# Sums inverted in slot 9, transposes one slot earlier, and the end of attention reordered: a fused attention and MoE kernel

## The chip, the cores and the metric

The kernel runs on one NeuronCore of a Trainium2 chip. Its engines run their own instruction streams in order and wait for one another by semaphores: TensorE (PE; PEld is its weight load), VectorE (DVE), ScalarE (ACT), GpSimd (POOL) and SyncE (SP), which here issues nearly all DMA transfers. The metric is the device time of one execution in microseconds; before the change the median of three runs is 876.56 us (876.08 to 878.52).

## The reference

```
q_assign = argmax(q_n . c_n);  k_assign = argmax(k_n . c_n)      # 16 clusters per head
mask     = q_assign == k_assign
scores   = where(mask, q k^T / sqrt(D), -1e9);  scores -= max(scores)
attn     = exp(scores);  attn /= sum(attn) + 1e-9;  x = attn v   # B=2, H=8, S=768, D=64
y        = relu(x w_in)^2 w_out                                  # 1536 tokens, 512 -> 2048 -> 512
out      = (h cos h) w2_out,  h = y w2_in
```

## The kernel before

**Attention.** The 16 heads are taken as eight pairs `n`, each of 768 queries by 768 keys. A pair has 12 slots (`SP`), one for each block of 128 keys (`kt`, 6) of each half of the queries (`hf`, 384 columns). Halves are numbered `hb` = 2n + hf, 0 to 15; slots run over all pairs as `g` = 0 to 95. In slot `g`:

- `scores` (L397) makes the transposed scores of one key block for both heads in eight matmuls and ScalarE takes the exponential into `p` (L413). The last two matmuls read `d["lq"]`, into whose outer rows `stage_max` has written the row maxima.
- `s_max` (L350) makes scores of the slot nine further on a second time, untransposed; VectorE takes their row maxima (L362).
- in odd slots `pv` (L427) multiplies the `p` of two earlier slots with V into `o_ps[hf]`.
- `add_up` (L415) adds the `p` of a half up in `acc`, on GpSimd, and for the very last half on VectorE.

`unit()` and `give()` hand out three PSUM units of two banks each in turn; whoever takes one waits for its last reader.

**What sets the order.** Three tables of (offset, place, function) say in which slot a step is issued and whether ahead of the slot's scores (PRE), behind its matmuls (PROD) or at its end (POST): `prep` (L806) for the preparation of a later pair, `prep_all` (L837) for the row maxima, `finish` (L846) for the end of a half. An offset in `prep` and `prep_all` counts from nine slots before the pair, one in `finish` from the half's first slot. Each engine, and SP's queue too, then works in this order.

- `prep`: load q and k (L226), transpose them (`transpose_in`, L244, six matmuls on `rawq` or `rawk`), copy (`full_copy`), round (`high_part`) and take the rest (`low_part`), then find each token's cluster (`sims`, `by_token`, `at_max`, `one_hot`) and move the operands of the second product (`stage_own`, `stage`, `stage_oh`: transfers `set<-set`, `ext<-set`, `ext<-ot`).
- `prep_all`: `stage_max` (L384) moves the row maxima of a half, `set<-mr`, two slots before that half's first.
- `finish`: `sums` (L442) sums `p` over the keys with a matrix of ones; `move_sums` (L453) copies the 128x192 result and gathers its four useful rows by four small transfers into a 64x12 tile `r`; three slots later `invert` (L473) adds 1e-9, inverts, writes `row` in DRAM and reads it back broadcast over 64 rows a head (`rb`); two slots later `divide` (L484) multiplies `o_ps` by `rb` into `x`, and `combine` (L488) splits `x` into the MoE's operands `xh` (ScalarE) and `xl` (GpSimd).

The last two halves do without DRAM: `sums_here` (L463) makes the sums on all 128 rows, `invert_here` (L470) inverts a 128x384 tile.

**MoE.** `moe` (L767) runs steps of one block of 512 tokens and one of 16 blocks of d_ff: `h_mm` (L610) and, two steps later, `y_mm` (L663), with elementwise work between. Weights are split on VectorE (L141, lines 157 to 161 and 153), two pieces in each of the last nine slots of attention and up to twelve in a step. `hooks` puts the end of attention into the first steps.

Of the kernel before, what the change touches and what calls it, by code (L numbers as in the profile page):

```python
# [9 lines left out]
F32 = mybir.dt.float32  # L10
# [4 lines left out]
AF = mybir.ActivationFunctionType  # L15
ALU = mybir.AluOpType
# [18 lines left out]
def tile_kernel(ctx: ExitStack, tc: tile.TileContext, q, k, v, centroids, w1i, w1o, w2i, w2o, out):  # L35
    nc = tc.nc
# [4 lines left out]
    P = 128  # L41
    NT = S // P
    HALF = S // 2
# [11 lines left out]
    R = D // 2  # L55
# [19 lines left out]
    eps = perm.tile([P, 1], F32, name="eps")  # L75
# [90 lines left out]
    ap = att.enter_context(tc.tile_pool(name="att", bufs=1))  # L166
# [11 lines left out]
    pairs = [(b, hp) for b in range(B) for hp in range(NP)]  # L178
    NPAIR = len(pairs)
    SP = 2 * NT  # L180
    NU = NPAIR * SP
# [7 lines left out]
    def unit():  # L189
        return free_units.pop(0)  # L190

    def give(u):
        free_units.append(u)
# [15 lines left out]
    def block(tiles, t):  # L209
        c, i = SPREAD[t]  # L210
        return tiles[c][:, S + i * P : S + (i + 1) * P]
# [138 lines left out]
    def s_max(u_):  # L350
        n, c = divmod(u_, SP)
        i, kh = divmod(c, 2)
        d = pd[n]
        u = unit()
        qs, ks = slice(i * P, (i + 1) * P), slice(kh * HALF, (kh + 1) * HALF)
        for p, (a, b) in enumerate(((d["hq"], d["hk"]), (xq[n % 2], xk[n % 2]))):
            for j in range(2):
                r = slice(j * D, (j + 1) * D)
                nc.tensor.matmul(u[:, j, :HALF], lhsT=a[r, qs], rhs=b[r, ks], start=(p == 0), stop=(p == 1))  # L359
        if c == 0:  # L360
            d["m"] = ap.tile([P, NT, 2, 2], F32, tag="m", name=f"m{n}", bufs=2)
        nc.vector.tensor_reduce(d["m"][:, i, :, kh], u[:, :, :HALF], AX, ALU.max)  # L362
        give(u)
# [30 lines left out]


    ptiles, accs = {}, {}
    def scores(u_):  # L397
        n, c = divmod(u_, SP)
        hf, kt = divmod(c, NT)
        d = pd[n]  # L400
        u = unit()
        qs, ks = slice(hf * HALF, (hf + 1) * HALF), slice(kt * P, (kt + 1) * P)
        i = n % 2
        lk, yk = d["lk"][:, ks], block(sets[n % 3], kt)
        ops = ((d["hk"][:, ks], d["hq"]), (lk, d["hq"]), (xk[i][:, ks], xq[i]), (yk, d["lq"]))
        for p, (a, b) in enumerate(ops):
            for j in range(2):
                r = slice(j * D, (j + 1) * D)
                nc.tensor.matmul(  # L409
                    u[:, j, :HALF], lhsT=a[r], rhs=b[r, qs], start=(p == 0), stop=(p == len(ops) - 1)  # L410
                )
        t = ptiles[u_] = ap.tile([P, 2, HALF], F32, tag="p", name=f"p{u_}", bufs=6)
        nc.scalar.activation(t, u[:, :, :HALF], AF.Exp, scale=SCALE)  # L413
        give(u)

    def add_up(u_):
        hb, kt = divmod(u_, NT)
        e = nc.vector if hb == 2 * NPAIR - 1 else nc.gpsimd
        if kt in (0, NT - 1):
            return  # L420
        if kt == 1:
            accs[hb] = ap.tile([P, 2, HALF], F32, tag="acc", name=f"acc{hb}", bufs=2)
        a = ptiles[u_ - 1] if kt == 1 else accs[hb]
        for j in range(2):
            e.tensor_tensor(accs[hb][:, j], a[:, j], ptiles[u_][:, j], ALU.add)  # L425
# [9 lines left out]
            )  # L435

    su, inv, rbs, xs = {}, {}, {}, {}
    GR = HALF // R
    QH = HALF // 2


# [10 lines left out]

    def move_sums(hb):  # L453
        u = su.pop(hb)
        t = ap.tile([P, QH], F32, tag="st", name=f"st{hb}")
        nc.scalar.copy(t, u[:, 0, :QH])
        give(u)
        r = inv[hb] = ap.tile([2 * R, GR], F32, tag="r", name=f"r{hb}", bufs=2)
        n = QH // GR
        for g in range(4):  # L460
            nc.sync.dma_start(r[g * n : (g + 1) * n], t[g * R : g * R + 1].rearrange("o (p c) -> o p c", c=GR))

    def sums_here(hb, u):  # L463
        for i, a in enumerate((accs.pop(hb), ptiles[NT * hb + NT - 1])):
# [5 lines left out]
    def invert_here(hb):  # L470
        nc.vector.reciprocal(rbs[hb], rbs[hb])

    def invert(hb):  # L473
        b, hp = pairs[hb // 2]
        r = inv.pop(hb)
        nc.vector.tensor_scalar(r, r, 1e-9, None, ALU.add)
        nc.vector.reciprocal(r, r)
        row = dram.tile([2, HALF], F32, tag="row", name=f"row{hb}", bufs=2)
        nc.sync.dma_start(row.rearrange("j (p c) -> (j p) c", c=GR), r)
        rb = rbs[hb] = ap.tile([P, HALF], F32, tag="rb", name=f"rb{hb}", bufs=2)  # L480
        for j in range(2):
            nc.sync.dma_start(rb[j * D : (j + 1) * D], row[j : j + 1, :].broadcast_to([D, HALF]))

    def divide(hb):  # L484
        x = xs[hb] = ap.tile([P, HALF], F32, tag="x", name=f"x{hb}", bufs=2)
        nc.vector.tensor_tensor(x, o_ps[hb % 2][:, :HALF], rbs.pop(hb), ALU.mult)  # L486

    def combine(hb):  # L488
        n, hf = divmod(hb, 2)
        b, hp = pairs[n]  # L490
        x = xs.pop(hb)
        c = hf * HALF
        while c < (hf + 1) * HALF:
            blk, off = divmod(b * S + c, TB)
            w = min((hf + 1) * HALF - c, TB - off)
            src = x[:, c - hf * HALF : c - hf * HALF + w]
            dst = xh[blk][:, hp, off : off + w]
            nc.scalar.copy(dst, src)
            nc.gpsimd.tensor_tensor(xl[blk][:, hp, off : off + w], src, dst.bitcast(F32), ALU.subtract)
            c += w  # L500

    def warm(count):
        for i in range(count):
            nc.tensor.matmul(o_ps[0][:, :P], lhsT=identb, rhs=identb, start=True, stop=True)
# [3 lines left out]
    st = prepp.tile([P, 4 * D], F32, name="st")  # L508
# [42 lines left out]
    for j in range(2):  # L551
        r = slice(j * D, (j + 1) * D)
# [214 lines left out]
    def moe(hooks):  # L767
# [36 lines left out]

    PRE, PROD, POST = range(3)
    prep = [  # L806
        (-13, PRE, load_raw, "qk"),
        (-10, PROD, transpose_in, "q"),
        (-10, POST, full_copy, "q"),
        (-9, PRE, high_part, "q"),  # L810
        (-9, POST, low_part, "q"),
        (-8, PROD, transpose_in, "k"),
        (-8, POST, full_copy, "k"),
        (-7, PRE, high_part, "k"),
        (-7, PROD, sims),
        (-7, POST, low_part, "k"),
        (-6, PROD, by_token),
        (-6, POST, stage_own),
        (-5, PROD, at_max),
# [26 lines left out]
    finish = [  # L846
        (8, PROD, sums),
        (9, PRE, move_sums),
        (12, PRE, invert),
        (14, PRE, divide),  # L850
        (14, POST, combine),
    ]
# [1 line left out]
    def run(g, where):  # L854
        for n in range(NPAIR):
            for r, w, f, *a in ([], prep_second, prep)[min(n, 2)] + prep_all:
                if g == SP * n - LEAD + r and w == where:
                    f(n, *a)
        for hb in range(2 * NPAIR - 2):
            for r, w, f in finish:  # L860
                if g == NT * hb + r and w == where:
                    f(hb)

    aux.extend(early_w.tile([P, DM], U32, name=f"aux{i}") for i in range(2))
    tops.extend(early_w.tile([P, DM], U32, name=f"top{i}") for i in range(2))
    last = 2 * NPAIR - 2
    loads = {8 * i: i for i in range(n_early)}
    loads.update({SP * (NPAIR - 2) + 1 + 2 * i: 6 + i for i in range(4)})
    loads.update({SP * (NPAIR - 1) + i: 9 + i for i in range(1, 7)})
    for g in range(-LEAD, NU):  # L870
        run(g, PRE)
        if 0 <= g < NU:
            scores(g)
        if 0 <= g + LEAD < NU:
            s_max(g + LEAD)
        if g % 2 == 1:
            for u_ in (g - 3, g - 2):
                if 0 <= u_ < NU:
                    pv(u_)
        run(g, PROD)  # L880
        run(g, POST)
        if 0 <= g - 1 < NU:
            add_up(g - 1)
        if g < -1:
            warm(WARM_STEP)
        if g in loads:
            load(0, *wanted[loads[g]], g + 4 - NU)
        if g >= SP // 2:
            if g < SP * (NPAIR - 1) - LEAD:
                count = 2 if g % SP in (1, 4, 7) else 0  # L890
            else:
                count = 2 if g >= NU - LEAD else 1
            for i in range(count):
                split_one(g - NU)
        if g == SP * (NPAIR - 1) - LEAD:
            prep_stack.close()
            mid = ctx.enter_context(tc.tile_pool(name="mid", bufs=1, side="right", reuse_waits="tile"))
            ews = mid.tile([P, 4 * TB], F32, name="ews")
            ewr = mid.tile([P, 6 * TB], F32R, name="ewr")
        if g == NU - 4:  # L900
            u = unit()
            sums_here(last, u)
            give(u)
        if g == NU - 2:
            invert_here(last)
            divide(last)
            combine(last)

    def load_mid():
        for i in wanted[16 : n_early + n_mid]:  # L910
# [2 lines left out]
    def load_late():  # L913
# [6 lines left out]

    moe({
        0: [lambda: pv(NU - 2), lambda: pv(NU - 1), lambda: sums_here(last + 1, units[2])],
        1: [load_mid],
        2: [lambda: invert_here(last + 1), lambda: divide(last + 1), lambda: combine(last + 1)],
        4: [load_late],
    })
# [28 lines left out]
```

## Time and profile before

| | us |
|---|---|
| median of 3 runs | 876.56 |
| profiled execution | 876.72 |
| its span | 875.0 |
| TensorE busy | 803.2 (92%) |
| VectorE busy | 581.7 (66%) |
| ScalarE busy | 355.7 (41%) |
| GpSimd busy | 184.4 (21%) |
| row maxima on VectorE, L362, 96 times | 91.6 |
| exponentials on ScalarE, L413, 96 times | 77.9 |

The span is the time from the first to the last instruction of one profiled execution; all times in rows count from its start. Busy time says little by itself: matmuls are pipelined, and an engine that waits in one stage and not in another has one share for both. What ended an idle stretch stands in brackets behind a row of the timeline. `SPq` rows are transfers as SyncE issues them; how long one takes to land is in the list of DMA issues.

### The profile page before, as it was taken

To read this page: it belongs to the slowest core of one execution; us is meant where nothing else is said; L and a number is where in the kernel's file an instruction comes from. 1 tells how busy PE (TensorE), PEld (TensorE's weight loads), DVE (VectorE), ACT (ScalarE), POOL (GpSimd) and SP (SyncE) were. 2 spreads that over 40 slices of the span, in tenths; PEclk is the share of its full clock that TensorE was granted. 3 is DMA by queue.
4 is the path that set the end of the run, shared out by engine and by line. 5 is a ranking of instruction groups with operands and counts; after the bars stand their busy time and mean duration, and the time that the engine had idled before them with its cause. 6 is when DMAs were issued, how large, how long until landed. Compare 5 with 4: busy or idle time off the path is not lost.

```text
span 875.0 us, 11831 instructions
## 1 busy us (share of the span) xinstructions
PE 803.2 (92%) x4453; PEld 596.8 (68%) x4453; DVE 581.7 (66%) x950; ACT 355.7 (41%) x591; POOL 184.4 (21%) x211
## 2 busy tenths in 40 slices
PE   6987977888787958999999999999899999999997
PEld 4654544545454526888888888888688888888886
DVE  5755554546555788869587731387999976667665
ACT  3344443534443433444444443444443433333332
POOL 5344445454434633200000000000222100000000
PEclk9999999999998898999999999999999999999999
DMA  4524253232314266010473000274100010001001
GB/s 109 124 76 102 55 121 87 60 91 57 83 51 133 65 210 234 2 49 1 134 227 121 1 0 1 65 228 145 46 1 0 1 49 1 0 1 49 1 0 49
DMA packets 75177, 61.84 MB, mean 71 GB/s; under 512 B 44144, under 2 KB 66416, under 8 KB 75120
## 3 DMA queue, kind: packets, MB, share of 16 engines
q1 hardware_dynamic: 73568, 60.70, 24.0%
q8 instruction: 35, 0.57, 0.3%
q10 hardware_dynamic: 1552, 0.39, 0.2%
q14 instruction: 22, 0.18, 0.1%
HBM read 47.87 MB, written 5.29 MB: 61 GB/s over the span
## 4 chain that ended last, share of the span: by engine, by line
PE 77%; DVE 7%; DMA 6%; ACT 4%; issue 2%; SPq 1%; DVEq 0%; ACTq 0%
PE unit L663 29%; PE unit L610 16%; PE o_ps L610 14%; PE o_ps L432 6%; PE unit L409 5%; DMA rb<-row 3%; PE unit L359 3%; DMA row<-r 2%; ACT p L413 2%; DVE m L362 2%; PE unit L249 1%; ACT fk L265 1%; PE unit L300 1%; PE unit L381 1%; SPq L345 1%
## 5 line engine op out<-in xcount | busy, mean ns | idle before, releaser
L610 PE MATMUL unit<-xh,w 128*128 128x512 f32 x400 | 134.3, 397 | 10.2 <-ACT p L413 6.8
L663 PE MATMUL unit<-ewr,w 128*128 128x512 f32 x576 | 141.9, 394 | 0.0
L663 PE MATMUL unit<-w,ewr 128*128 128x512 f32 x576 | 140.1, 392 | 1.8 <-ACT ewr L644 0.7
L362 DVE TENSOR_REDUCE m<-unit 128x2 f32<-128x768 f32 x96 | 91.6, 955 | 69.1 <-PE unit L359 68.3
L663 PEld LDWEIGHTS unit<-w,ewr 128*128 128x128 f32 x576 | 107.9, 188 | 26.8 <-ACT ewr L644 1.1
L663 PEld LDWEIGHTS unit<-ewr,w 128*128 128x128 f32 x576 | 107.9, 187 | 25.8
L610 PE MATMUL o_ps<-xh,w 128*128 128x512 f32 x368 | 121.2, 390 | 0.0
L413 ACT ACTIVATE p<-unit 128x768 f32<-128x768 f32 x96 | 77.9, 813 | 68.8 <-PE unit L409 66.6
L648 POOL TENSOR_TENSOR ewr<-ews,ewr 128x512 fp32r<-128x512 f32 x24 | 31.7, 1322 | 331.7 <-ACT ewr L644 297.5
L610 PEld LDWEIGHTS unit<-xh,w 128*128 128x128 f32 x400 | 76.2, 190 | 29.5 <-ACT p L413 7.4
L425 POOL TENSOR_TENSOR acc<-acc,p 128x384 f32<-128x384 f32 x90 | 92.9, 1066 | 5.6 <-ACT p L413 5.6
L409 PE MATMUL unit<-set,set 64*128 64x384 f32 x512 | 81.3, 373 | 10.3 <-ACT p L413 7.1
L648 DVE TENSOR_TENSOR ewr<-ews,ewr 128x512 fp32r<-128x512 f32 x72 | 49.5, 688 | 56.4 <-ACT ewr L627 51.4
L432 PE MATMUL o_ps<-p,rawv 128*64 128x384 f32 x384 | 82.3, 555 | 0.9 <-DVE x L486 0.8
L610 PEld LDWEIGHTS o_ps<-xh,w 128*128 128x128 f32 x368 | 69.1, 188 | 15.3
L610 PE MATMUL unit<-xl,w 128*128 128x512 f32 x200 | 79.2, 396 | 0.0
L635 ACT ACTIVATE ews<-ews,hpi 128x512 f32<-128x512 f32 x48 | 34.8, 725 | 102.9 <-DVE ews L634 102.9
L610 PE MATMUL o_ps<-xl,w 128*128 128x512 f32 x184 | 72.0, 391 | 0.0
L409 PEld LDWEIGHTS unit<-set,set 64*128 64x128 f32 x512 | 44.1, 191 | 33.2 <-ACT p L413 14.1
L359 PE MATMUL unit<-set,set 64*128 64x384 f32 x192 | 37.8, 387 | 26.2 <-DVE m L362 26.2
L153 DVE SCALAR_TENSOR_TENSOR w<-aux,aux 128x512 fp32r<-128x512 f32 x64 | 50.0, 781 | 1.8
L432 PEld LDWEIGHTS o_ps<-p,rawv 128*64 128x64 f32 x384 | 25.3, 148 | 34.4 <-issue 32.3
(129 smaller groups left out, 1072.5 us busy)
## 6 DMA issues: line engine op xcount, KB each, us to landing
wraw<-in_moe_w_in_dram SPq DMA_DIRECT2D x32, 512.0 KB, 4.5
wraw<-in_moe_w_out_dram SPq DMA_DIRECT2D x32, 512.0 KB, 4.5
rawq<-in_q_dram SPq DMA_DIRECT2D x8, 384.0 KB, 4.6
ext<-set SPq DMA_DIRECT2D x32, 96.0 KB, 2.1
rawv<-in_v_dram SPq DMA_DIRECT2D x8, 384.0 KB, 4.1
out_dram<-outs SPq DMA_DIRECT2D x12, 256.0 KB, 2.1
rawk<-in_k_dram SPq DMA_DIRECT2D x7, 384.0 KB, 5.1
rb<-row SPq DMA_DIRECT2D x28, 96.0 KB, 2.9
```

Source lines behind the costliest of these rows:

```text
L153: ve.scalar_tensor_tensor(w[:, 1], restf, 2.0**-20, power.bitcast(F32), ALU.mult, ALU.mult)
L249: nc.tensor.transpose(u[:, h, c * P : (c + 1) * P], raw[n, x][:, t].rearrange("p j d -> p (j d)"), ident)
L359: nc.tensor.matmul(u[:, j, :HALF], lhsT=a[r, qs], rhs=b[r, ks], start=(p == 0), stop=(p == 1))
L362: nc.vector.tensor_reduce(d["m"][:, i, :, kh], u[:, :, :HALF], AX, ALU.max)
L409: nc.tensor.matmul(u[:, j, :HALF], lhsT=a[r], rhs=b[r, qs], start=(p == 0), stop=(p == len(ops) - 1))
L413: nc.scalar.activation(t, u[:, :, :HALF], AF.Exp, scale=SCALE)
L425: e.tensor_tensor(accs[hb][:, j], a[:, j], ptiles[u_][:, j], ALU.add)
L432: nc.tensor.matmul(o_ps[hf][j * D : (j + 1) * D, :HALF], lhsT=raw[n, "v"][:, kt, j, :], rhs=t[:, j], start=(kt == 0), stop=(kt == NT - 1),)
L610: nc.tensor.matmul(ph, lhsT=w[:, a, :], rhs=x[blk][:, a, :], start=(a == i == 0), stop=(a == KD - 1 and i == 2))
L635: nc.scalar.activation(e2, e2, AF.Sin, bias=hpi)
L648: e.tensor_tensor(al, e2, ah.bitcast(F32), ALU.subtract)
L663: nc.tensor.matmul(y, lhsT=a, rhs=b, start=(idx in opens and i == 0), stop=(idx in closes and i == 2))
```

## The change

- `finish`: `invert` stands at the end of slot 9 of a half, not ahead of slot 12. `move_sums` writes the sums with 1e-9 added straight into a 128x192 tile `r`; the four gathering transfers, the tile `st` and the 64x12 addition are gone. `invert` inverts all 128 rows and sends every 32nd of them to `row`.
- `prep`: load, transposes, copies, rounding and rests of q and k are one slot earlier. `sims` and all behind it stay.
- `add_up`: the half last but one is added on VectorE too.
- `invert_here`, `divide` and `combine` of the half last but one move from the end of slot 94 into the MoE's step 1.

```diff
-        e = nc.vector if hb == 2 * NPAIR - 1 else nc.gpsimd
+        e = nc.vector if hb >= last else nc.gpsimd
...
     def move_sums(hb):
         u = su.pop(hb)
-        t = ap.tile([P, QH], F32, tag="st", name=f"st{hb}")
-        nc.scalar.copy(t, u[:, 0, :QH])
+        r = inv[hb] = ap.tile([P, QH], F32, tag="r", name=f"r{hb}", bufs=2)
+        nc.scalar.activation(r, u[:, 0, :QH], AF.Identity, bias=eps)
         give(u)
-        r = inv[hb] = ap.tile([2 * R, GR], F32, tag="r", name=f"r{hb}", bufs=2)
-        n = QH // GR
-        for g in range(4):
-            nc.sync.dma_start(r[g * n : (g + 1) * n], t[g * R : g * R + 1].rearrange("o (p c) -> o p c", c=GR))
...
     def invert(hb):
-        b, hp = pairs[hb // 2]
         r = inv.pop(hb)
-        nc.vector.tensor_scalar(r, r, 1e-9, None, ALU.add)
         nc.vector.reciprocal(r, r)
         row = dram.tile([2, HALF], F32, tag="row", name=f"row{hb}", bufs=2)
-        nc.sync.dma_start(row.rearrange("j (p c) -> (j p) c", c=GR), r)
+        nc.sync.dma_start(row.rearrange("j (h c) -> (j h) c", h=2), r[0:P:R])
...
-        (-10, PROD, transpose_in, "q"),
+        (-11, PROD, transpose_in, "q"),
...
-        (12, PRE, invert),
+        (9, POST, invert),
...
-        if g == NU - 2:
-            invert_here(last)
-            divide(last)
-            combine(last)
...
-        1: [load_mid],
+        1: [lambda: invert_here(last), lambda: divide(last), lambda: combine(last), load_mid],
```

SP's queue from slot 9 of an even half on, before: `mr` are the row maxima, `ot` the one-hot clusters, `r`, `row` and `rb` the sums on their way.

```order
L461 DMA r_680<-st_678 16x1x12 x4
L284 DMA set_0_124<-set_1_125 64x256
L284 DMA set_1_125<-set_1_125 64x256
L284 DMA set_2_126<-set_1_125 64x2x128
L391 DMA set_2_122<-mr_719 32x384 x2
L290 DMA ext_1_129<-set_1_125 32x768 x2
L290 DMA ext_0_128<-set_2_126 32x768 x2
L345 DMA ext_0_128<-ot_765 32x384 x2
L345 DMA ext_1_129<-ot_765 32x384 x2
L479 DMA row_779<-r_680 64x12
L482 DMA rb_781<-row_779 64x384 x2
L224 DMA rawq_820<-in_q_dram 128x12x64
```

The same place of the same queue with the change:

```order
L284 DMA set_0_124<-set_1_125 64x256
L284 DMA set_1_125<-set_1_125 64x256
L284 DMA set_2_126<-set_1_125 64x2x128
L473 DMA row_713<-r_678 4x192
L476 DMA rb_715<-row_713 64x384 x2
L391 DMA set_2_122<-mr_720 32x384 x2
L290 DMA ext_1_129<-set_1_125 32x768 x2
L290 DMA ext_0_128<-set_2_126 32x768 x2
L345 DMA ext_0_128<-ot_766 32x384 x2
L345 DMA ext_1_129<-ot_766 32x384 x2
L224 DMA rawq_793<-in_q_dram 128x12x64
```

`row` and `rb` have moved from behind the eight `ext` transfers to ahead of `set<-mr`, and the gathering transfers are gone.

VectorE in the same slots, before: `m` are the row maxima of `s_max`, `mx` the best similarity of each token, `x` the divided output.

```order
L371 TENSOR_REDUCE m_675<-m_530 128x6
L362 TENSOR_REDUCE m_530<-unit_67 128x2
L315 TENSOR_REDUCE mx_710<-unit_65 128x24
L362 TENSOR_REDUCE m_530<-unit_65 128x2
L329 TENSOR_TENSOR eq_741<-sc_659,unit_66 128x384
L362 TENSOR_REDUCE m_530<-unit_65 128x2
L337 TENSOR_SCALAR ot_765<-unit_66,oh_above,oh_scale 128x384
L476 TENSOR_SCALAR r_680<-r_680 64x12
L477 RECIPROCAL r_680<-r_680 64x12
```

And with the change:

```order
L371 TENSOR_REDUCE m_675<-m_530 128x6
L362 TENSOR_REDUCE m_530<-unit_65 128x2
L315 TENSOR_REDUCE mx_705<-unit_67 128x24
L471 RECIPROCAL r_678<-r_678 128x192
L362 TENSOR_REDUCE m_530<-unit_67 128x2
L329 TENSOR_TENSOR eq_742<-sc_660,unit_66 128x384
```

The reciprocal has grown from 12 to 192 columns and stands two maxima earlier, right behind `mx`.

ScalarE at the end of attention, before: the last exponentials `p`, the operands `xh` of the half last but one, and the first elementwise step of the MoE (`ews`).

```order
L413 ACTIVATE p_3175<-unit_67 128x768
L498 CAST xh_102<-x_3182 128x256
L498 CAST xh_103<-x_3182 128x128
L413 ACTIVATE p_3196<-unit_65 128x768
L468 ACTIVATE rb_3226<-unit_67,eps 128x384
L625 ACTIVATE ews<-unit_65 128x512
```

And with the change:

```order
L414 ACTIVATE p_3091<-unit_67 128x768
L414 ACTIVATE p_3105<-unit_65 128x768
L464 ACTIVATE rb_3135<-unit_67,eps 128x384
L619 ACTIVATE ews<-unit_65 128x512
L620 ACTIVATE ews<-ews 128x512
L621 CAST ewr<-ews 128x512
L152 CAST w_6_0_3142<-top_311 128x512
L492 CAST xh_102<-x_3161 128x256
L492 CAST xh_103<-x_3161 128x128
```

The two `xh` pieces have moved from ahead of the last exponential to behind the MoE's first elementwise step.

## Rows read from the trace of the kernel before

**Rows 1.** Windows: us, then busy us of each engine, PEclk, DMA share, GB/s

```profile
78.00:104.00 26.00, 23.43 (x201) 14.95 (x201) 15.86 (x24) 13.35 (x23) 14.18 (x15) 1.00 0.30 76
112.00:117.00 5.00, 4.55 (x23) 2.41 (x25) 1.52 (x3) 1.83 (x5) 4.85 (x6) 0.66 0.85 157
282.00:290.00 8.00, 6.31 (x29) 3.77 (x31) 4.82 (x6) 2.60 (x6) 6.61 (x7) 0.57 0.12 42
```

**Rows 2.** Waits from 75 to 260 us: us in total, times, longest us

```profile
PE unit L359 <- DVE m L362: 15.3, 4, 4.0
PE unit L409 <- ACT p L413: 5.8, 10, 1.1
PE unit L300 <- ACT p L413: 5.3, 5, 1.1
...
DVE x L486 <- DMA rb<-row: 23.1, 9, 4.8
```

**Rows 3.** Timeline of SP's issues from slot 10: start us, us, queue, line, transfer

```profile
98.28 1.20 SPq L391 DMA_DIRECT2D set<-mr  x2
...
102.58 2.42 SPq L345 DMA_DIRECT2D ext<-ot  x4
105.09 1.11 SPq L479 DMA_DIRECT2D row<-r  x1
107.45 1.12 SPq L482 DMA_DIRECT2D rb<-row  x2
...
109.25 0.67 SPq L224 DMA_DIRECT2D rawq<-in_q_dram  x1
```

**Rows 4.** Timeline of ScalarE at the end of attention

```profile
327.35 0.60 ACT L498 CAST xh<-x 128x256 fp32r<-128x256 f32 x2 [5.83 <-DVE x L486]
```

**Rows 5.** Timeline of VectorE

```profile
96.55 0.56 DVE L315 TENSOR_REDUCE mx<-unit 128x24 f32<-128x384 f32 x1 [1.22 <-PE unit L313]
...
110.97 0.56 DVE L486 TENSOR_TENSOR x<-o_ps,rb 128x384 f32<-128x384 f32 x1 [4.49 <-DMA rb<-row]
...
113.53 0.96 DVE L362 TENSOR_REDUCE m<-unit 128x2 f32<-128x768 f32 x1 [0.93 <-PE unit L359]
...
324.08 2.55 DVE L471 RECIPROCAL rb<-rb 128x384 f32<-128x384 f32 x1
```

**Rows 6.** Timeline of TensorE: the readers of `lq`, and waits near the end

```profile
102.39 0.34 PE L409 MATMUL unit<-set,set 64*128 64x384 f32 x2
...
121.61 0.34 PE L409 MATMUL unit<-set,set 64*128 64x384 f32 x2
...
283.69 0.69 PE L359 MATMUL unit<-set,set 64*128 64x384 f32 x2 [3.22 <-DVE m L362]
...
309.06 0.97 PE L409 MATMUL unit<-set,set 64*128 64x384 f32 x6 [2.97 <-DMA set<-mr]
...
328.72 0.80 PE L610 MATMUL unit<-xh,w 128*128 128x512 f32 x1 [6.77 <-ACT p L413]
```

**Rows 7.** Groups by line: count | busy us, mean ns | idle before

```profile
L477 DVE RECIPROCAL r<-r 64x12 f32<-64x12 f32 x14 | 3.1, 220 | 0.5
...
L425 DVE TENSOR_TENSOR acc<-acc,p 128x384 f32<-128x384 f32 x6 | 3.1, 550 | 0.0
```

**Rows 8.** DMA issues: count, KB each, median us from issue to landing

```profile
rawq<-in_q_dram SPq DMA_DIRECT2D x8, 384.0 KB, 4.6
...
rb<-row SPq DMA_DIRECT2D x28, 96.0 KB, 2.9
...
set<-mr SPq DMA_DIRECT2D x32, 48.0 KB, 1.9
...
row<-r SPq DMA_DIRECT2D x14, 3.0 KB, 1.7
```

More of the change, by code (lines that the diff above doesn't have):

```diff
@@ L396, in tile_kernel @@
     ptiles, accs = {}, {}
+    last = 2 * NPAIR - 2
     def scores(u_):
@@ L437, in tile_kernel @@
     su, inv, rbs, xs = {}, {}, {}, {}
-    GR = HALF // R
     QH = HALF // 2
@@ L806, in tile_kernel @@
     prep = [
-        (-13, PRE, load_raw, "qk"),
-        (-10, PROD, transpose_in, "q"),
[L809 to L814, printed above, removed]
+        (-14, PRE, load_raw, "qk"),
+        (-11, PROD, transpose_in, "q"),
+        (-11, POST, full_copy, "q"),
+        (-10, PRE, high_part, "q"),
+        (-10, POST, low_part, "q"),
+        (-9, PROD, transpose_in, "k"),
+        (-9, POST, full_copy, "k"),
+        (-8, PRE, high_part, "k"),
+        (-8, POST, low_part, "k"),
         (-7, PROD, sims),
-        (-7, POST, low_part, "k"),
         (-6, PROD, by_token),
@@ L865, in tile_kernel @@
     tops.extend(early_w.tile([P, DM], U32, name=f"top{i}") for i in range(2))
-    last = 2 * NPAIR - 2
     loads = {8 * i: i for i in range(n_early)}
```

## The prediction

> **What bounds the kernel now.** I read the chain of waits and the granted clock by stretch first, then the waits of a steady stretch, then the timelines of SP, ScalarE, VectorE and TensorE around one wait. The MoE part, from 328.72 us on [rows 6], is one unbroken run of matmuls that the change does not touch; all that can change lies before it. A pair of heads takes 12 slots, some 38 us. Once in each pair TensorE stands still: in the 185 us from 75 to 260 the maxima's matmuls (L359) waited 15.3 us in 4 times for VectorE [rows 2], 3.8 us each. VectorE itself was held by `divide` (L486), which waited for the landing of `rb`: 4.49 us at 110.97 [rows 5]; six such gaps repeat, the last at 264.01. Behind the gap the granted clock is down: 0.66 over 112 to 117 us, so 0.34 x 5.00 = 1.7 us lost, against 1.00 from 78 to 104 us [rows 1].
>
> Why is `rb` late? The sums are ready in slot 9 and `divide` stands in slot 14. But `invert` is in slot 12, and SP, which issues all these transfers in order, has the eight `ext` transfers in front of it: `ext<-ot` from 102.58 for 2.42 us, `row<-r` at 105.09, `rb<-row` at 107.45 [rows 3]. With 2.9 us to landing for the second `rb` [rows 8] that is 110.9. The wait is a place in SP's queue, not a transfer's length.
>
> **The change part by part.** The profiled execution took 876.72 us, its span 875.0; the median is 876.56, so the sum is made against 876.72 and needs no correction.
>
> *Sums inverted in slot 9.* Gone are per half four `r<-st` transfers, an addition and a 64x12 reciprocal (220 ns [rows 7]). New is a reciprocal of 128x192 on VectorE. Its price lies between that 0.22 us and the 128x384 one, 2.55 us [rows 5]; linear in the columns between these two rows, (2.55 - 0.22) x 180/372 + 0.22 = 1.35 us, which I take. ScalarE's Identity with a bias replaces a copy of the same shape at no cost on the path.
> In the even half of a pair it runs behind `mx`, 96.55 + 0.56 [rows 5], and would end at 98.5. `row<-r` goes out then, lands 1.7 us later at 100.2 [rows 8], and the second `rb` (issued 0.6 us behind the first) lands at about 103.7. `divide` began to wait at 110.97 - 4.49 = 106.5: its wait goes, 6 x 3.8 = 22.8 us, and the slow stretches behind five of these, 5 x 1.7 = 8.5 us (the sixth is counted with the tail).
>
> *What is late next.* SP waits in order for `row` to land, and `set<-mr` now stands behind `rb`. Before it was issued at 98.28 [rows 3]; now after 100.2 + 1.12 = 101.4. Its second transfer starts 0.6 later and lands 1.9 us after that [rows 8]: 103.9. The scores of slot 0 read it with their last two matmuls, at 102.39 [rows 6]. TensorE waits 1.5 us that it did not wait before. For the odd half the same chain starts behind the maximum at 113.53 + 0.96 [rows 5]: reciprocal to 115.8, `row` landed 117.6, `rb` issued to 118.7, `set<-mr` landed 121.2. Its reader was at 121.61 [rows 6] after a slow-clock stretch worth up to 1.7 us, so the wait lies between 0 and 1.4 us; I take 1.0, since most of that stretch had matmuls to run. Cost: 6 x 1.5 + 5 x 1.0 = 14.0 us (the first pair has no odd half yet).
> The `ext` transfers move back by some 3 us; their readers in slot 3, some 6 us behind slot 0, still find them landed, with about 1 us to spare. VectorE gets about 2 x 1 us more in each pair, which its idle time hides (busy 15.86 of 26 us [rows 1]). At worst the reciprocal pushes back the next maximum, and with it the unit of memory that TensorE writes next, by half its length, 0.7 us a half: 11 x 0.7 = 7.5 us, which I keep for the range.
>
> The Trainium skill (VectorE: DVE Perf Modes, First, the fixed hardware budget) says that a reciprocal is an iterative divide with a repeat count of 8; as an estimate from it and its 0.96 GHz, 192 columns take 1.6 us and 384 take 3.2. The trace has 2.55 us for 384, so it is quicker than that here. By the page each new wait would grow by 0.25 us, 3 us in all; the sum goes by the row.
>
> *Transposes one slot earlier.* They leave the slot that also holds the four P.V products' eight matmuls and come into one without. ScalarE's copy and rounding of the transposed tile then run while TensorE has P.V to do. What they cost in the slots after them were TensorE's waits for ScalarE's exponentials: 5.8 us at L409 and 5.3 us at L300 in five pairs [rows 2], 2.2 us a pair. I count them all as gone: 6 x 2.2 = 13.2 us; the bounds are 0 and 13.2. The raw loads are asked for one slot earlier too (109.25 before [rows 3], about 107.5 in the same frame now) and land 4.6 us later [rows 8], 112; the transposes come at about 113. They are nearly as late as their reader.
>
> *The last two halves.* Additions of one more half move to VectorE: 8 at 0.55 us [rows 7], 4.4 us, hidden under the twelve last slots, where GpSimd's same additions fall away. `invert_here`, `divide` and `combine` of the last but one half leave ScalarE's queue in front of the last exponential. There TensorE waited 6.77 us up to 328.72 [rows 6]; that exponential stands behind `xh` at 327.35 [rows 4], which waited for a 2.55 us reciprocal at 324.08 [rows 5] behind VectorE's splits. Now it waits for its scores alone: -6.4 us. In the MoE's step 1 the same work lies beside the matmuls of steps 0 and 1; its tokens are read in step 8 at the earliest. The first step's slow clock (TensorE had just been idle) is taken half away, -1.7.
> In the tail from 266 to 302 us go a wait of 3.22 us at 283.69 [rows 6] and slow stretches behind it and behind 264.01 (0.43 x 8.00 = 3.4 [rows 1], and 1.7); two new waits of 1.5 and 1.6 come, and 1.0 because additions now stand before the last maxima: -4.2. The wait of 2.97 us for `set<-mr` at 309.06 [rows 6] stays, since the slots there are short.
>
> Sum: -22.8 - 8.5 + 14.0 - 13.2 = -30.5 for the pairs; -4.2 - 6.4 - 1.7 = -12.3 for the end; -42.8 in all: 833.9, forecast **834 us**.
>
> **The rivals.**
> *No new wait.* `set<-mr` is in time after all, because TensorE reaches slot 0 later than I think or because `row` with its four long rows lands sooner. For it: the reader is only 1.5 us ahead. Against: the chain reciprocal, `row`, `rb`, `set<-mr` has no slack in it. All 14.0 and 3.1 us come back: 817 us.
> *The new waits stop the clock.* Each of some 12 waits is followed by a half-speed stretch as behind 110.97, 1.7 us: 834 + 20 = 854. For it: a clock of 0.66 behind a wait of 3.8 us [rows 1, 2]. Against: from 78 to 104 us, with waits of 1.1 us in it [rows 1, 2], it stayed at 1.00.
> *It does not do what it says.* `divide` still waits, since `rb` is late for a reason other than its place on SP; only the end and the transposes gain: 876.7 - 13.2 - 12.3 = 851.
> *Slower.* SP becomes the bound: it stands idle while `row` lands, twice a pair, with `set<-mr`, eight `ext` and the raw loads behind it. If `row<-r` and `set<-mr` each take twice their median (3.4 and 3.8 us, 3.6 more in a chain), the waits become 5.1 and 4.6 us a half and each drags 1.7 us of slow clock: 7.2 + 3.4 = 10.6 more a pair than forecast, 6 x 10.6 = 64: 898 us. It decides when the two chains together cost over 9 us a pair; the medians speak against it.
>
> **How the numbers follow.** Forecast 0.60; no new wait 0.17; clock stopped 0.13; not doing what it says 0.05; slower 0.05. The forecast's own bounds are 826 (new waits half as long) and 847 (no gain from the transposes). The range runs from 815, just under the case without a wait, to 853, at the case of the stopped clock. A measurement of this kernel tells 0.3%, 2.6 us, from no change. Only the slower case ends above the time of before, and a milder form of it ends near it: faster 0.94, same 0.02, slower 0.04.
>
> **What would show it.** Right: VectorE's `x` no longer waits for `rb`; in each pair TensorE waits at L410 for `set<-mr`, about 1.5 and 1.0 us; the granted clock stays near 1.00 over a pair; the exponentials of a slot 3 follow one another after about 33 us; the MoE's first matmul starts near 287 us. Wrong: the 128x192 reciprocal takes over 1.7 us; the transposes wait for `rawq`; s_max's second pair waits for `ext`; the first MoE steps wait for VectorE.

## The result, and the profile after

The changed kernel takes 839.56 us (median of 4 runs, 838.24 to 840.22) against 877.09 for the kernel before, run beside it: a ratio of 0.9569 [0.9549, 0.9589]. The forecast was 834 (815 to 853). One run among the experiments below, of `no_trans`, took 953.21 us at a mean granted clock of 0.79 and is left out. The profiled execution took 838.24, its span is 836.5 us (875.0 before). First the head of the page of the kernel after (busy us of each engine):

```profile
span 836.5 us, 11709 instructions
PE 794.2 (95%) x4453; PEld 591.7 (71%) x4453; DVE 592.6 (71%) x944; ACT 357.2 (43%) x591; POOL 177.3 (21%) x203
```

TensorE's busy time has fallen by 9.0 us although it runs the same 4453 matmuls. Its granted clock has risen, from 0.974 to 0.993 of full speed in the mean, which shortens them; matmuls behind the new waits take longer, as the comparison with `inv10` shows below. The other 29.5 us of the span are idle time that is gone.

The steady part is best compared between equal places. From the exponential of slot 3 in one pair to the same one five pairs on, the kernel before and the kernel after have these windows (us, busy us of PE, PEld, DVE, ACT and POOL, PEclk, DMA share, GB/s). Before:

```profile
75.05:266.19 191.14, 159.34 (x1287) 95.99 (x1285) 103.28 (x155) 83.23 (x143) 90.40 (x97) 0.95 0.32 78
```

After, and behind it two later windows near the end:

```profile
71.44:236.50 165.06, 154.46 (x1289) 93.20 (x1289) 115.02 (x146) 84.56 (x143) 91.34 (x98) 1.00 0.38 92
...
246.00:251.00 5.00, 4.80 (x26) 2.96 (x26) 3.31 (x5) 1.62 (x2) 0.00 (x0) 0.66 0.91 268
...
280.00:287.00 7.00, 6.79 (x34) 3.52 (x34) 3.75 (x8) 3.11 (x5) 0.00 (x0) 0.66 0.55 215
```

A pair now takes 33.0 us instead of 38.2, and over five pairs TensorE's idle time falls from 31.8 to 10.6 us, its busy time by 4.9. The granted clock is 1.00 throughout (2.4 GHz); the stretches at 0.66 of [rows 1] are gone from here, and two have come near the end.

TensorE's waits in the two stretches of five pairs (us in total, times, longest us), before:

```profile
PE unit L359 <- DVE m L362: 19.2, 5, 4.0
```

The two rows for the exponentials are as in [rows 2], 5.8 and 5.3 us. And after:

```profile
PE unit L410 <- DMA set<-mr: 6.6, 8, 1.4
...
PE unit L410 <- ACT p L414: 0.8, 5, 0.2
PE unit L249 <- DMA rawq<-in_q_dram: 0.6, 1, 0.6
```

The three waits of [rows 2] have gone or shrunk to 0.8, and one that was not there has come: for `set<-mr`, the row maxima. VectorE's timeline after has no bracket at `x` where [rows 5] had 4.49 us, and shows the new reciprocal:

```profile
90.91 1.35 DVE L471 RECIPROCAL r<-r 128x192 f32<-128x192 f32 x1
...
101.98 0.55 DVE L480 TENSOR_TENSOR x<-o_ps,rb 128x384 f32<-128x384 f32 x1
```

SP's issues behind it, which answer to [rows 3] (start us, us, line, transfer), and the matmuls of an odd and of this even half that read `set<-mr`:

```profile
92.28 0.55 SPq L473 DMA_DIRECT2D row<-r  x1
93.92 1.14 SPq L476 DMA_DIRECT2D rb<-row  x2
95.15 1.21 SPq L391 DMA_DIRECT2D set<-mr  x2
96.46 2.45 SPq L290 DMA_DIRECT2D ext<-set  x4
```

```profile
79.53 0.64 PE L410 MATMUL unit<-set,set 64*128 64x384 f32 x2 [0.55 <-DMA set<-mr]
...
97.71 0.62 PE L410 MATMUL unit<-set,set 64*128 64x384 f32 x2 [1.27 <-DMA set<-mr]
```

`rb` is ahead of the `ext` transfers now. Between `row` and `rb` SP does nothing for 1.1 us, since `rb` reads what `row` writes, and `set<-mr` goes out behind both. In [rows 6] these matmuls had no wait.

TensorE's timeline from the sixth of those pairs to the MoE:

```profile
246.20 0.61 PE L410 MATMUL unit<-set,set 64*128 64x384 f32 x2 [3.44 <-DMA set<-mr]
...
262.13 0.65 PE L410 MATMUL unit<-set,set 64*128 64x384 f32 x2 [1.19 <-DMA set<-mr]
...
280.21 1.49 PE L410 MATMUL unit<-set,set 64*128 64x384 f32 x6 [4.93 <-DMA set<-mr]
...
292.64 0.50 PE L604 MATMUL unit<-xh,w 128*128 128x512 f32 x1
```

The MoE's first matmul is 36.1 us earlier than in [rows 6], without its wait of 6.77 us and at full clock. But two waits of 3.44 and 4.93 us for `set<-mr` stand ahead of it, and the windows at 0.66 above lie right behind them. Where does the span's 38.5 us come from? Up to the exponential of slot 75: 266.19 - 236.50 = 29.7. From there to the MoE: 62.5 before, 56.1 after, 6.4. The MoE: 546.3 before, 543.9 after, 2.4.

### The profile page after: what moved, and what is told of

The parts are those of the page before. It is cut to its first block, busy times and chain, and to the rows that moved or that the text cites. A ratio compares the mean times of both kernels' runs of the same rounds, so it can differ in the third digit from the quotient of the medians.

```text
span 836.5 us, 11709 instructions
## 1 busy us (share of the span) xinstructions
PE 794.2 (95%) x4453; PEld 591.7 (71%) x4453; DVE 592.6 (71%) x944; ACT 357.2 (43%) x591; POOL 177.3 (21%) x203
## 4 chain that ended last, share of the span: by engine, by line
PE 77%; DVE 7%; DMA 6%; SPq 3%; ACT 2%; issue 2%; DVEq 0%; ACTq 0%
PE unit L657 29%; PE unit L604 16%; PE o_ps L604 14%; PE unit L410 7%; PE o_ps L433 5%; DMA set<-mr 4%; PE unit L359 3%; DMA row<-r 2%; DVE r L471 2%; SPq L476 1%; PE unit L448 1%; DVE ews L626 1%; PE unit L249 1%; DVE ews L625 1%; SPq L345 1%
## 5 line engine op out<-in xcount | busy, mean ns | idle before, releaser
L604 PE MATMUL unit<-xh,w 128*128 128x512 f32 x400 | 132.5, 392 | 3.4 <-ACT ews L619 1.9
L410 PE MATMUL unit<-set,set 64*128 64x384 f32 x512 | 87.4, 377 | 19.7 <-DMA set<-mr 17.3
L426 POOL TENSOR_TENSOR acc<-acc,p 128x384 f32<-128x384 f32 x84 | 86.7, 1067 | 3.2 <-ACT p L414 3.2
L410 PEld LDWEIGHTS unit<-set,set 64*128 64x128 f32 x512 | 48.0, 187 | 53.6 <-DMA set<-mr 22.5
L433 PE MATMUL o_ps<-p,rawv 128*64 128x384 f32 x384 | 74.6, 510 | 0.0
L158 DVE SCALAR_TENSOR_TENSOR aux<-wraw,aux 128x512 f32<-128x512 uint32 x64 | 46.3, 723 | 1.8
L433 PEld LDWEIGHTS o_ps<-p,rawv 128*64 128x64 f32 x384 | 23.8, 139 | 30.6 <-issue 30.5
```

Source lines behind the costliest of these rows:

```text
L158: cost(690, lambda: ve.scalar_tensor_tensor(restf, low, 2.0**-32, rest, ALU.mult, ALU.add)),
L410: nc.tensor.matmul(u[:, j, :HALF], lhsT=a[r], rhs=b[r, qs], start=(p == 0), stop=(p == len(ops) - 1))
L433: nc.tensor.matmul(o_ps[hf][j * D : (j + 1) * D, :HALF], lhsT=raw[n, "v"][:, kt, j, :], rhs=t[:, j], start=(kt == 0), stop=(kt == NT - 1),)
L604: nc.tensor.matmul(ph, lhsT=w[:, a, :], rhs=x[blk][:, a, :], start=(a == i == 0), stop=(a == KD - 1 and i == 2))
```

## The experiments

Each ratio is against the kernel before, run on the same chip (medians 877.0 to 878.3).

**p11.** In the kernel before, `invert` one slot earlier, nothing else. This tests whether the wait came from the place of `invert` in the order, on SP's queue above all.

```diff
-        (12, PRE, invert),
+        (11, PRE, invert),
```

> Kernel before with one number changed: invert ahead of slot 11 instead of slot 12, so that row and rb stand ahead of the eight ext transfers in SP's queue; the four gathering transfers, the 64x12 inversion, the transposes and the end stay. Theory A (the wait was a place in SP's queue): divide stops waiting, 6 x 3.8 and the slow stretches behind go, ext lands some 3 us later and costs up to 1 us a pair: 845 to 852 us. Theory B (the gain comes from the shorter path of the sums, without gathering): rb stays late, 872 to 877 us.

850.71 us, 0.9694 [0.9661, 0.9726]. Its waits from 75 to 260 us:

```profile
DVE x L486 <- DMA rb<-row: 11.1, 8, 2.7
...
PE unit L359 <- DVE m L362: 3.4, 6, 1.2
```

One number in a table brings 26 us: with `row` and `rb` ahead of the `ext` transfers, TensorE's wait for the maxima falls from 15.3 [rows 2] to 3.4 us, though the small gathering transfers are all still there. That the place of `invert` in the order made `rb` late is shown. But the edit moves two things. VectorE's inversion in the kernel before, and the inversion and SP's issues in `p11`:

```profile
102.66 0.22 DVE L477 RECIPROCAL r<-r 64x12 f32<-64x12 f32 x1
```

```profile
97.40 0.22 DVE L477 RECIPROCAL r<-r 64x12 f32<-64x12 f32 x1
```

```profile
95.56 1.21 SPq L391 DMA_DIRECT2D set<-mr  x2
97.65 0.48 SPq L479 DMA_DIRECT2D row<-r  x1
```

Counted from the issue of `set<-mr`, `row` went out after 6.8 us before [rows 3] and goes out after 2.1 here. Before, the inversion was done at 102.88 and `row` was issued at 105.09: 2.2 us of the 4.7 lay in SP's queue. The other 2.5 are the inversion's own later place on VectorE. No run moves one without the other.

**sums_only.** The kernel before with the part on the sums alone.

```diff
-        t = ap.tile([P, QH], F32, tag="st", name=f"st{hb}")
-        nc.scalar.copy(t, u[:, 0, :QH])
+        r = inv[hb] = ap.tile([P, QH], F32, tag="r", name=f"r{hb}", bufs=2)
+        nc.scalar.activation(r, u[:, 0, :QH], AF.Identity, bias=eps)
...
-        (12, PRE, invert),
+        (9, POST, invert),
```

> Kernel before with the sums' part alone: sums written with 1e-9 added into 128x192, inverted at the end of slot 9. Theory A: the divide waits go, waits for set<-mr of about 1 us a half come, the last exponential still waits 6 us for xh: 850 to 856 us. Theory B': parts work only together, above 865 us.

855.94 us, 0.9761 [0.9723, 0.98]: 21 us, and 5 slower than `p11`, which moves `invert` less far. The waits from 75 to 260 us point to the cause, which `inv10` tests below:

```profile
PE unit L409 <- DMA set<-mr: 12.2, 11, 3.6
```

The wait for the maxima is gone; 12.2 us of waits for `set<-mr` stand in its place (0.5 in `p11`).

**trans_only.** The kernel before with the earlier transposes alone: in `prep`, every offset from `load_raw` to `low_part` one less.

```diff
-        (-10, PROD, transpose_in, "q"),
+        (-11, PROD, transpose_in, "q"),
```

> Kernel before with the transposes' part alone. Theory A: TensorE's waits of 1.06 us for exponentials behind the transposes go, two a pair, 6 x 2.2: 863 to 868 us. Rival: the time is only moved to the wait for rb in slot 2, 875 to 878 us.

874.41 us, 0.9967 [0.9948, 0.9986], from 10 runs against 19 of the kernel before. Its waits from 75 to 260 us:

```profile
DVE x L486 <- DMA rb<-row: 25.2, 9, 5.1
...
PE unit L359 <- DVE m L362: 16.3, 4, 4.4
...
PE unit L409 <- DVE m L362: 6.4, 5, 1.8
...
PE unit L409 <- ACT p L413: 0.8, 5, 0.2
```

The waits for exponentials are gone, 11.1 us down to 0.8, and only 2.7 us are won. TensorE merely comes sooner to the place where `rb` holds up the maxima, and waits there longer, 6.4 us of it at a place where it did not wait before.

**no_trans.** The kernel after with this part alone undone (the diff above the other way).

> Changed kernel with the transposes' part undone (sums and end stay). Theory A (the transposes pay only once divide no longer waits for rb): TensorE's waits behind the transposes are back, some 2 us a pair, 848 to 853 us, 9 to 13 us above the changed kernel although the part alone gave 3 us. Rival (the part is worth the same 3 us everywhere): 841 to 844 us.

851.50 us (the middle of 847.52, 851.50 and 851.75), 0.9703 [0.9678, 0.9728]: some 12 us more than the kernel after, and 8.0 even at its fastest. Its waits from 45 to 245 us:

```profile
PE unit L410 <- DMA set<-mr: 9.8, 11, 1.5
PE unit L300 <- ACT p L414: 6.3, 6, 1.1
PE unit L410 <- ACT p L414: 5.2, 12, 1.1
```

The same edit is worth 2.7 us while `rb` is late and some 12 once it isn't. The forecast's 13.2 was the second number.

**end_only.** The kernel before with the end's part alone.

```diff
-        e = nc.vector if hb == 2 * NPAIR - 1 else nc.gpsimd
+        e = nc.vector if hb >= last else nc.gpsimd
...
-        if g == NU - 2:
-            invert_here(last)
-            divide(last)
-            combine(last)
...
-        1: [load_mid],
+        1: [lambda: invert_here(last), lambda: divide(last), lambda: combine(last), load_mid],
```

> Kernel before with the end's part alone: additions of the last two halves on VectorE, the last but one half combined in the MoE's step 1. Theory A: the wait of 6.8 us in front of the MoE's first matmul goes and its first step runs at the full clock: 867 to 870 us. Rival: VectorE, with 4.4 us more in these slots, gives it back: 874 to 878 us.

874.65 us, 0.9963 [0.9946, 0.998], also from 10 runs against 19. The wait ahead of the MoE is gone, but VectorE and TensorE, in this order, wait elsewhere:

```profile
319.46 0.56 DVE L487 TENSOR_TENSOR x<-o_ps,rb 128x384 f32<-128x384 f32 x1 [6.83 <-DMA rb<-row]
```

```profile
320.07 1.51 PE L433 MATMUL o_ps<-p,rawv 128*64 128x384 f32 x8 [2.00 <-DVE x L487]
...
324.94 0.51 PE L611 MATMUL unit<-xh,w 128*128 128x512 f32 x1 [0.33 <-ACT p L414]
```

The MoE starts 3.8 us earlier than in [rows 6], not 6.4: the `rb` of the half before is late here too, and its `x` holds P.V's output.

**no_end.** The kernel after with this part undone.

> Changed kernel with the end's part undone (sums and transposes stay). Theory A: the last exponential waits for xh again and the MoE's first step runs slow, 844 to 849 us. Rival: the end is worth the 2.5 us that it gave alone, 841 to 843 us.

844.66 us, 0.9626 [0.9603, 0.9648], 5.1 more. In its timeline of TensorE the MoE's first matmul waits again, and runs at half the clock (granted 0.50 from 296 to 300 us, and 0.79 us for what takes 0.50 above):

```profile
296.07 0.79 PE L604 MATMUL unit<-xh,w 128*128 128x512 f32 x1 [3.62 <-ACT p L413]
```

Alone the three parts bring 21.2, 2.7 and 2.5 us, 26.4; together 37.5. The late `rb` hid much of the other two: `trans_only` and `end_only` show the waits for it.

**loads.** What is behind the two long waits of the tail? In SP's issues of the kernel after, a weight load stands between `rb` and `set<-mr` there:

```profile
240.65 1.13 SPq L476 DMA_DIRECT2D rb<-row  x2
241.84 0.58 SPq L132 DMA_DIRECT2D wraw<-in_moe_w_out_dram  x1
242.51 1.18 SPq L391 DMA_DIRECT2D set<-mr  x2
...
275.60 0.59 SPq L132 DMA_DIRECT2D wraw<-in_moe_w_in_dram  x1
276.28 1.17 SPq L391 DMA_DIRECT2D set<-mr  x2
```

From the start of the issue to the end of TensorE's wait it is 3.7 and 3.9 us (246.20 - 242.51, 280.21 - 276.28); between 95.15 and 97.71 it was 2.6. These are the row maxima of the halves that begin in slots 78 and 90. The experiment moves the load (512 KB) of slot 75 to slot 76 and those of slots 87 to 90 one slot on.

```diff
-    loads.update({SP * (NPAIR - 2) + 1 + 2 * i: 6 + i for i in range(4)})
-    loads.update({SP * (NPAIR - 1) + i: 9 + i for i in range(1, 7)})
+    loads.update({SP * (NPAIR - 2) + g: 6 + i for i, g in enumerate((1, 4, 5, 7))})
+    loads.update({SP * (NPAIR - 1) + g: 10 + i for i, g in enumerate((1, 2, 4, 5, 6, 7))})
```

> Changed kernel with the weight loads of slots 75 and 87 moved one slot back, so that none is issued between rb and set<-mr. Theory A (the two long waits at the end, 3.4 and 4.9 us, are long because 0.5 MB is issued and moved ahead of set<-mr): they fall to about 1.5 and 3 us and the slow stretches behind may go: 832 to 836 us. Rival: they are long since the slots at the end are short: 838 to 841 us.

833.37 us, 0.9486 [0.9463, 0.9509], 6.2 less than the kernel after. TensorE's waits where 3.44 and 4.93 stood:

```profile
244.91 0.68 PE L410 MATMUL unit<-set,set 64*128 64x384 f32 x2 [1.50 <-DMA set<-mr]
...
275.42 1.68 PE L410 MATMUL unit<-set,set 64*128 64x384 f32 x6 [2.58 <-DMA set<-mr]
```

The load ahead of `set<-mr` made the waits longer by 1.94 and 2.35 us; the rest of them, 1.50 and 2.58, has another source. The slow stretch behind the first is gone too (granted clock 1.00 from 244.9 to 250 us), the one behind the second is not (0.50 from 275.25 to 281.75).

**inv10.** In the kernel after, `invert` one half-step later, so that `set<-mr` is issued ahead of `row` and `rb`.

```diff
-        (9, POST, invert),
+        (10, PRE, invert),
```

> Changed kernel with invert ahead of slot 10, behind stage_max, instead of at the end of slot 9: set<-mr goes out before row and rb. Theory A (what is left between 834 and the measured time are waits for set<-mr behind row and rb): these waits go in the pairs and shrink at the end, 819 to 827 us. Rival: the wait moves on to the ext transfers or back to divide, 836 to 842 us.

819.49 us, 0.9326 [0.9304, 0.9348]: 20 us better than the kernel after, and with `inv10_loads` the fastest. SP's issues, in the place that was shown for the kernel after:

```profile
90.46 1.21 SPq L391 DMA_DIRECT2D set<-mr  x2
91.77 0.55 SPq L473 DMA_DIRECT2D row<-r  x1
93.41 1.14 SPq L476 DMA_DIRECT2D rb<-row  x2
```

Its waits from 40 to 300 us:

```profile
DVE x L480 <- DMA rb<-row: 1.8, 1, 1.8
...
PE unit L249 <- DMA rawq<-in_q_dram: 2.1, 3, 1.6
```

TensorE waits for `set<-mr` only once in the whole span, for 0.2 us (17.3 us in 13 times in the kernel after), and `rb`, half a slot later, is still in time but once. The MoE starts 20.4 us earlier (272.26). Up to there, in the columns of the windows above, the kernel after:

```profile
0.00:292.64 292.64, 259.96 (x2134) 158.99 (x2134) 200.97 (x277) 135.24 (x222) 140.91 (x176) 0.98 0.39 99
```

And `inv10`, with its five pairs from slot 3 to slot 3 behind it:

```profile
0.00:272.26 272.26, 252.29 (x2133) 156.73 (x2133) 197.19 (x271) 135.30 (x222) 141.04 (x176) 0.99 0.41 106
...
69.41:227.38 157.97, 150.75 (x1285) 92.36 (x1285) 112.47 (x145) 84.62 (x142) 91.05 (x97) 1.00 0.39 96
```

TensorE's idle time falls from 32.7 to 20.0 us: 17 us of waits for `set<-mr` are gone, and some 4 us of idle time have come elsewhere, in part for `rawq` and `ext<-ot` (1.5 us). Its busy time falls by 7.7 us. Some 3.9 of these are the two slow stretches, 0.34 x (4.80 + 6.79). The rest shows in the five pairs, where the granted clock is 1.00 in both kernels: 150.75 us busy against 154.46, 3.7 less (some 0.5 of it may be the four matmuls fewer on record, 1285 against 1289). So a new wait costs more than its idle time. Behind a wait of 0.95 us the kernel after takes 2.48 us from the matmuls that waited to P.V (196.51 to 198.99); `inv10` takes 1.90 for the same matmuls without a wait (94.78 to 96.68). The MoE itself gives 2.1 back (546.0 against 543.9).

**inv10_loads.** Both edits.

> Both edits together. Theory A: 816 to 823 us, the fastest; no wait for set<-mr over 1 us but at the last half. Rival: no faster than the better of the two.

819.69 us, 0.9328 [0.9305, 0.9352], the same as `inv10`: with `set<-mr` ahead of the round trip a load behind `rb` holds up nothing. The 6.2 us of `loads` and the 20 of `inv10` are the same waits, not a sum.

**p11_all.** The kernel before with `invert` in slot 11 and the other two parts of the change, but the old small sums.

```diff
-        (12, PRE, invert),
+        (11, PRE, invert),
...
-        (-10, PROD, transpose_in, "q"),
+        (-11, PROD, transpose_in, "q"),
...
+        1: [lambda: invert_here(last), lambda: divide(last), lambda: combine(last), load_mid],
```

> Kernel before with invert ahead of slot 11, the transposes' part and the end's part, but with the gathered 64x12 sums of before. Theory A (place in the queue decides, not the form of the sums): 828 to 840 us, as fast as the changed kernel. Theory B (the form decides): over 845 us.

834.86 us, 0.9498 [0.947, 0.9525], 4.7 less than the kernel after. So a gain as large does not need the four gathering transfers and the small reciprocal to go. Its waits from 45 to 300 us:

```profile
DVE x L487 <- DMA rb<-row: 9.1, 5, 4.7
...
PE unit L410 <- DMA set<-mr: 3.2, 1, 3.2
```

`rb` is late again in five halves, where it was so once in `inv10`; the two kernels lie 15.4 us apart.

## Why the prediction was right

By its steps, in the order of its sum:

- *Divide's wait.* Forecast 3.8 us a pair gone; measured 19.2 us in five pairs, all of it, and `x` waits for `rb` nowhere in the pairs. The cause, the place of `invert` in the order, is shown by `p11`. The prediction put it down to SP's queue alone; the queue was 2.2 us of the 4.7 by which `row` was late, and the inversion's own slot on VectorE the rest.
- *The slow stretches.* Forecast 1.7 us each, 8.5 in five. `inv10` has neither the slow stretches nor the new waits, and there TensorE is busy 8.6 us less in five pairs than in the kernel before (159.34 - 150.75). By the granted clock it is some 9.6 (0.05 x 191.14, with a rounded 0.95). The term was right. That the kernel after shows a fall of only 4.9 (159.34 - 154.46) is the next term's doing.
- *The new waits.* The place was right, L410 for `set<-mr`, and the size near. They are 6.6 us idle in five pairs and up to 3.7 us of longer matmuls behind them (154.46 - 150.75), 10.3 together, against 5 x (1.5 + 1.0) = 12.5. The idle time is 1.1 us in the mean of the even halves (0.94 to 1.42) where I took 1.5, and in the odd halves 0.55, 0.25, 0.19 and twice nothing where I took 1.0. The longer matmuls were not in the working, and their time made up for most of that: this part is luck.
- *The transposes.* Forecast 13.2; undoing them costs some 12. In five pairs the waits for exponentials fell from 11.1 to 0.8. Right, but only in company: alone they bring 2.7, which the working did not say.
- *The pairs together.* -29.7 against -30.5. In the five pairs the same terms give -19.0 - 8.5 - 11.0 + 12.5 = -26.0 as forecast and -26.1 measured (191.14 - 165.06). Term by term it is -19.2 - 8.6 - 10.3 + 10.3, and 1.7 of idle time that the forecast did not have, 0.6 of it for `rawq`, one of its signs of being wrong. The terms are right to within some 2 us; that the sum is right to 0.1 is luck. A slot 3 follows the last after 33.0 us, as forecast.
- *The tail and the start of the MoE.* This is the step that was off, by 4.2 us: -4.2 and -6.4 forecast up to the MoE's first matmul, -6.4 measured. The new wait at slot 78 was taken as 1.5 and the last one, at slot 90, as the 2.97 us of [rows 6]; they are 3.44 and 4.93, with a slow stretch behind each. So the MoE starts at 292.64 and not near 287. I had carried the delay of the pairs into the tail without reading what else SP issues there. `loads` shows that it is the weight load between `rb` and `set<-mr`: with it moved the two waits are 1.50 and 2.58, near the forecast's sizes, and 6.2 us come back.
- *The MoE.* -2.4 against -1.7 for its first step. The prediction called it one unbroken run of matmuls; it has 9.6 us of idle time in either kernel, and the 2.4 are busy time (536.7 to 534.3), with the granted clock from 0.99 to 1.00.
- *The reciprocal.* 1.34 to 1.35 us, the 1.35 of the line between two rows. The Trainium skill (VectorE: DVE Perf Modes, First, the fixed hardware budget) would have it at 1.6 by its repeat count of 8; the trace decides against that estimate. ScalarE's Identity, taken at no cost, is 0.1 us longer than the copy (means 0.42 and 0.32).

Sum: -29.7 - 6.4 - 2.4 = -38.5 against -42.8. Of the rivals, *the new waits stop the clock* holds in part: behind waits of up to 1.4 us the granted clock stays at 1.00, behind 3.44 and 4.93 us it is 0.66, and behind the 2.58 us of `loads` it falls to half as well. *No new wait* is what `inv10` makes: its 819.49 lies near the 817 that was worked out for this case, so its working is borne out, though the price put on the waits, 17.1 us, was 20.1 as measured, and more of it lay in the tail than was forecast. That the change does not do what it says, and that SP becomes the bound, are out: `x` no longer waits for `rb`, and the new waits cost some 2 us a pair, not over 9, with `set<-mr` 2.2 us from issue to landing at its median.

What stays open: why the wait for `set<-mr` is shorter in odd halves than in even ones by more than the working gave; why TensorE's matmuls take longer behind a wait at a granted clock of 1.00; and how much of `p11_all`'s distance from `inv10` is the lateness of `rb` and how much the 3.2 us wait for `set<-mr`; no run separates these.

## What to carry to other kernels

In a queue that works in order, rank transfers by how near their reader is in time, and put a step that must wait in the queue (a round trip through DRAM) behind whatever has a nearer reader: half a slot's difference was worth 20 us here, more than half of what the whole change brought. Before adding up parts, ask which of them lies behind the same stall, since what is freed ahead of a stall is waited away in it. And where a pattern is carried from the steady part to the end, read the queue of the end by itself.

## What was not expected of the hardware

A transfer of 48 KB issued right behind a load of 512 KB on the same queue let its reader go 3.7 to 3.9 us after its issue began; issued right behind the 96 KB `rb` transfers it was 2.6 (97.71 - 95.15). With the loads moved, the same two transfers took 2.3 and 2.2 (244.91 - 242.59, 275.42 - 273.18 in `loads`). In the list of DMA issues of the kernel after (count, KB each, median us to landing) it is 2.2:

```profile
set<-mr SPq DMA_DIRECT2D x32, 48.0 KB, 2.2
```

The small transfer pays for the large one ahead of it, though SP itself is through with the load after 0.58 us (at 241.84).

The matmuls behind a short wait cost time too, though the granted clock stayed at 1.00: 0.58 us more behind a wait of 0.95 us (2.48 against 1.90 above).
